# Forms of the hidden DFT matrices stored unsplit and split where the column transforms load them

## The chip, the cores and the metric

One core of one Trainium2 chip runs the kernel. The metric is device time of one execution in microseconds. The core has five engines that each work through their own list of instructions in order and wait for each other by semaphores: TensorE (PE: matmuls, PEld: its weight loads), VectorE (DVE), ScalarE (ACT), GpSimd (POOL) and SyncE (SP), whose list is mostly DMA issues.

## What is computed

```
xn = layernorm(x)                          # x: 2048 x 640, eps 1e-5, no scale or shift
a  = xn @ wr.T ;  b = xn @ wi.T            # wr, wi: 640 x 640, DFT over the hidden axis
y  = cr @ a - ci @ b                       # cr, ci: 2048 x 2048, DFT over the sequence
out = x + y + (gelu(xn @ w1 + b1) @ w2 + b2)   # w1: 640 x 1536, w2: 1536 x 640
```

All data are fp32.

## The kernel before, in words

**Split products.** TensorE takes fp32r operands. Each fp32 operand is split in two: a high half, a copy into fp32r (`high`, L189, on ScalarE), and a low half, what is left (`low`, L192, on VectorE). `product` (L301) then makes three matmuls per pair of 128-row tiles: high by high, high by low, low by high. A matmul is 128x128 weights against 128x512 columns.

**Stages.** The program runs in this order. The MLP for the first rows, then six `pair` steps (L1121), each with two hidden units of two row blocks, then the rest of the MLP. Then the sequence transform over eight blocks. Each is a Strassen-like scheme of NW = 7 products (`w` = 0 to 6) of sums of sub-blocks of cr and ci with sums of rows of xn. After the sixth and after the eighth block follows a column stage (kind "y" in `stages`, L544), which applies the hidden DFT, wr and wi, to the sums of two blocks, again as 7 products. The last column stage also takes the last four units of the MLP along with w2.

**Column stages.** A product `w` runs over ND = 5 chunks of 128 rows of its matrix form; the chunks come in the order 0, 2, 1, 3, 4. An *entry* (`hidden_entry`, L1877) handles two chunks, or one (`u` = 2), or the two late units (`u` = 3, last stage only). The matrix form of a chunk is 3 x 128 columns wide in products 0, 1, 2 and 6 and 2 x 128 in products 3, 4 and 5 (`GWIDE`), so a chunk is nine or six matmuls. The seven forms are: the first two and the last of five blocks of 128 columns of wr, then of wi, then sums of such blocks, and for product 6 the middle two of wi with the last one negated.

**Where the forms are made.** During pairs 1 to 5 and shortly after, wr and wi are loaded in five pieces (`load_w`, L397), transposed on VectorE (`turn_w`, L406), and turned into forms (`prep_w`, L447). `put_w` (L414) splits each form, ScalarE for the high half and VectorE for the low half, into a staging tile (`wst` and free tiles of other pools), and a DMA from GpSimd's queue writes both halves to DRAM (`wits`, seven tensors).

**Where they are used.** `load_g` (L1668) brings a chunk's two halves back with one DMA on SP's queue into one of 7 places (first column stage) or 13 (last): three in the tile `ws`, two each in the two `raw` tiles, which the sequence transform has left, and in the last stage six in the tiles `xab`. `hidden_entry` issues the load for a place when the chunk in it has been used, so a load is some 7 or 13 chunks ahead. Three chunks are loaded during the sequence block before the stage. No engine but TensorE touches the chunk after that.

**What sets the order.** The order is written by hand. For each entry the loop at the end of the program (L1928 on) emits the matmuls, then work left over (`later`, `pre`), then `form` for the entry three further on (a copy on ScalarE and a subtraction on VectorE, 128x1024, into one of three slots `as`, five in the last stage), then `post`: the work of `hidden_beside` (L1686) or `beside` on VectorE and ScalarE, with output DMAs. In the last column stage the outputs of three column ranges leave from GpSimd's queue (`store` with `nc.gpsimd`), and `late_form` (L1451) splits pieces of w2 on ScalarE and VectorE.

Of the kernel before, what the change touches and what calls it, by code (L numbers as in the profile page):

```python
# [15 lines left out]
P = 128  # L16
# [11 lines left out]
def kernel(  # L28
# [74 lines left out]
    ys = [dram.tile([NT, P, NB, c1 - c0], F32, name=f"ys{k}") for k, (c0, c1) in enumerate(YCOLS)]  # L103

    GWIDE = (3, 3, 3, 2, 2, 2, 3)
    wits = [dram.tile([ND, P, 2, n * P], F32, name=f"wit{w}") for w, n in enumerate(GWIDE)]
    NK = 4
    forms_ab = dram.tile([NK, P, 2, 10 * P], F32, name="forms_ab")
    forms_c = dram.tile([NK, P, 2, 7 * P], F32, name="forms_c")
# [79 lines left out]
    def high(h, s):  # L189
        nc.scalar.activation(h, s, AF.Copy)  # L190
# [220 lines left out]
            A.pop(("wraw", m)).rearrange("p (q c) i -> p q c i", q=Q),  # L411
        )

    def put_w(w, j, main, odd=None, negative=False):  # L414

        n = GWIDE[w] * P
        st, last = A["wst"], j >= ND - 2
        if w in (0, 1, 6):
            k = w % 5 if w < 6 else 2
            t = st[:, k * 6 * P : (k + 1) * 6 * P].rearrange("p (a b) -> p a b", a=2)  # L420
            parts = [(t, 0, n)]
        else:
            name = f"wst{w}_{j}"
            if w in (2, 3):
                t = rows.tile([P, 2, 2 * P], F32R, tag="yt", bufs=2, name=name)
            elif not last:
                t = early.tile([P, 2, 2 * P], F32R, tag="w2r", bufs=3, name=name)
            elif w == 4:
                t = mr.tile([P, 2, 2 * P], F32R, tag="zt" if j < ND - 1 else "ab", bufs=2, name=name)
            else:  # L430
                lo = 12 * P if j < ND - 1 else 0
                t = st[:, lo : lo + 4 * P].rearrange("p (a b) -> p a b", a=2)
            parts = [(t, 0, 2 * P)]
            if w == 2:
                parts.append((st[:, 18 * P : 20 * P].rearrange("p (a b) -> p a b", a=2), 2 * P, n))
        to = parts[-1][0][:, :, -P:]
        split(t[:, 0, : 2 * P], t[:, 1, : 2 * P], main)
        if odd is not None and not negative:
            split(to[:, 0], to[:, 1], odd)
        elif odd is not None:  # L440
            h, l = to[:, 0], to[:, 1]
            nc.scalar.activation(h, odd, AF.Copy, scale=-1.0)
            nc.vector.scalar_tensor_tensor(l, odd, -1.0, h.bitcast(F32), op0=ALU.mult, op1=ALU.subtract)
        for t, c0, c1 in parts:
            nc.gpsimd.dma_start(wits[w][j][:, :, c0:c1], t.bitcast(F32))

    def prep_w(j, k):  # L447

        (r1, r2, r4), (i1, i2, i4) = (
            (A["wt", m][:, : 2 * P], A["wt", m][:, 2 * P : 4 * P], A["wt", m][:, 4 * P :]) for m in range(2)  # L450
        )

        if k == 0:
            put_w(0, j, r1, r4)
            put_w(1, j, i1, i4)
            add(r4, r4, i4)
        if k == 1:
            put_w(6, j, i2, i4, True)
            add(i2, i2, r2)
            put_w(2, j, i2, r4)  # L460
            add(r2, r1, r2, ALU.subtract)
            add(r1, i2, r1, ALU.subtract)
            add(i1, i1, r1, ALU.subtract)
        if k == 2:
            put_w(3, j, r1)
            put_w(4, j, i1)
            put_w(5, j, r2)

    def add(dst, a, b, op=ALU.add):
        nc.vector.tensor_tensor(dst, a, b, op=op)  # L470
# [559 lines left out]
    def beside_pair(k, at):  # L1030

        if k == 0:

            if at == 5:
                bias_sum(0, 0)
                turn_x("t30", "a")
                turn_x("t31", "a")
                A["ot0"] = turn_sum(0, 0, rows, "yt", True)
                split_x("t30")
                split_x("t31")  # L1040
            if at == 6:
                turn_x("t40", "a")
                turn_x("t41", "a")
                split_x("t40")
                split_x("t41")
                bias_sum(0, 1)
                load_w(0, 0)
                load_w(1, 0)
            if at == 8:
                A["ot1"] = turn_sum(0, 1, rows, "yt", True)  # L1050
            if at == 4:
                add_sum(0, 0, A["ot0"])
                add_sum(0, 1, A["ot1"])
                store_sums(0, 0)
                bias_sum(0, 2)
            return
        j = k - 1
        if k == 1:
            if at == 2:
                add_sum(0, 2, turn_sum(0, 2, rows, "yt", True))  # L1060
            if at == 5:
                finish(0, 3, 4)
                store_sums(0, 1, 2)
            if at == 3:
                A["wst"] = zo_tile("wst", (P, NB * DQ), F32R)
        if k == LASTK and at == 4:
            split_unit(2 * NF + 1, units[1])
        if at == {1: 7, LASTK: 4}.get(k, 6):
            turn_w(0, j)
            turn_w(1, j)  # L1070
        if k == 1:
            steps = {7: (0,), 4: (1,)}
        elif k == 2:
            steps = {5: (-1,), 7: (0,), 4: (1,)}
        elif k == LASTK - 1:
            steps = {5: (-1,), 8: (0,)}
        elif k == LASTK:
            steps = {5: (-2,), 8: (-1,)}
        else:
            steps = {5: (-1,), 8: (0,), 4: (1,)}  # L1080
        if at == (7 if k == 1 else 3) and j + 1 < ND:
            load_w(0, j + 1)
            load_w(1, j + 1)
        if k == 2 and at == 2:
            home = rows_in("rt2")
            A["rows_3"] = home
            for c in range(3 * NC, 4 * NC):
                load_x(c, home=home)
        if k == LASTK - 1 and at in (7, 4):
            for c in (12, 13) if at == 7 else (14, 15):  # L1090
                ln_stats(c)
                scale_by_power(c)
        if k == LASTK and at == 8:
            split_unit(2 * NF, units[0])
        for n in steps.get(at, ()):
            prep_w(*((j - 1, 3 + n) if n < 0 else (j, n)))
        if k == LASTK and at == 2:
            for i in range(3):
                load_unit(i)
        if k == LASTK and at == 8:  # L1100
            A["gs"] = place("xab1", (P, 5, TB), F32)
            for i in range(3, 8):
                load_unit(i)
            for c in range(3 * NC, 4 * NC):
                ln_apply(c)
        if k == LASTK and at == 7:
            A["s1"] = place("xab2", (P, ND, TB), F32)
        if k == LASTK and at == 4:
            Z["z"] = place("xab3", (P, NB, DQ), F32)
            put_z(Z["z"], A["rows_3"], nc.gpsimd, nc.sync)  # L1110
            split_unit(2 * NF + 2, units[2])
# [374 lines left out]
    def beside(h, t, n):  # L1486
# [108 lines left out]
        else:  # L1595
# [12 lines left out]
                A["g", b] = [A["ws"][:, k] for k in range(3)]  # L1608
            if second and 3 <= n < 6:
                post.append(lambda: load_g(b, n - 3))  # L1610
            if n == 6 and p == 2:

                def load_yo():
                    yo[t] = out_pool.tile([P, NB, DQ], F32, tag="zo", bufs=1, name=f"yo{t}")
                    for q in range(Q):
                        nc.sync.dma_start(yo[t][q * B : (q + 1) * B], rows_of(x, t)[:, :, q * DQ : (q + 1) * DQ])

                post.append(load_yo)
# [49 lines left out]
    def load_g(b, i):  # L1668
        if i >= NW * ND:
            return  # L1670
        w, c = G[i]
        n = GWIDE[w] * P
        places = A["g", b]
        k = i % len(places)
        if b < len(blocks) - 1 and w == NW - 1:


            k = (i - 2 if c == CHUNKS[1][0] else i) % len(places)
            if c in CHUNKS[0]:
                k = CHUNKS[0].index(c)  # L1680
                places = {k: fr_tile((P, 6 * P), f"u{2 - k}_{sets[blocks[b]]}", f"gr{k}_{b}", F32R)}
        g = places[k][:, : 2 * n].rearrange("p (a b) -> p a b", a=2)
        GT[b, i] = g
        nc.sync.dma_start(g.bitcast(F32), wits[w][c])

    def hidden_beside(b, n):  # L1686

# [241 lines left out]
    for kind, what in stages:  # L1929
        b = blocks.index(what) if kind == "s" else b  # L1930
        count = NW * steps_in((kind, what)) if (kind, what) != stages[-1] else NW * NLATE
        for n in range(first, first + count):
            w, u = entries[n][2:]
            if kind == "s":
                sequence_entry(n, what, w, u)
                pre, post = beside(*what, n - first)
            else:
                hidden_entry(n, b, w, u)
                pre, post = hidden_beside(b, n - first)
            for f in later:  # L1940
                f()
            later.clear()
            for f in pre:
                f()
            while made <= n + 3 + min(max(n - LASTY + 2, 0), 2):
                form(made)
                made += 1
            for f in post:
                f()
        first += count  # L1950
        if n + 1 < len(entries):
            X, Y, Z = Y, Z, X
# [47 lines left out]
```

## Time and profile before

| | |
|---|---|
| time, median of 3 runs | 847.53 us (846.95 to 848.32) |
| the profiled execution | 847.4 us, its span 845.6 us |
| first column stage, by the timeline | 596.0 to 657.2 us |
| last column stage, by the timeline | 755.1 to 841.1 us |
| pairs and the making of the forms | about 100 to 210 us |

A row of a group names the line, the engine, the operation, the tiles (out<-in), the shapes and the count; after the bar come busy time in us, the mean of one in ns, and the idle time of that engine just before, with what ended it. A row of the timeline begins with start and duration in us. A row of the windows names the stretch, its length, and the busy time of PE, PEld, DVE, ACT and POOL with the number of instructions in brackets, the granted clock, the share of DMA and GB/s. A row of one line or tile has the shortest, median and longest duration in ns. In the waits, "A <- B: us, times, longest" says that A stood idle until B.

### The profile page before, as it was taken

The page shows a single profiled execution, that of the slowest core. Times are in us where ns is not written, and L with a number is a line of the kernel's source. Part 1 is how long each engine was busy: PE and PEld are TensorE (multiplying, and loading weights), DVE is VectorE, ACT ScalarE, POOL GpSimd, SP SyncE. Part 2 cuts the span into 40 slices and gives each one's busy share as a digit, 9 for nine tenths or more (in the row PEclk, how much of TensorE's full clock was granted, in tenths as well). Part 3 has the DMA queues.
Part 4 walks back from the last instruction along what each step waited for, and adds up shares of the span by engine and source line. Part 5 has one row for each costly group of instructions (what it writes and reads, how often), then busy time and mean ns, then how long its engine had stood idle before and what let it go on. Part 6 is the DMA issues. An engine that isn't in the chain of part 4 may idle for free.

```text
span 845.6 us, 10713 instructions
## 1 busy us (share of the span) xinstructions
PE 839.2 (99%) x3719; PEld 695.5 (82%) x3719; DVE 694.3 (82%) x920; ACT 374.6 (44%) x546; POOL 90.5 (11%) x166
## 2 busy tenths in 40 slices
PE   9999999999999999999999999999999999999997
PEld 7888888888888888888888888888888888888886
DVE  6969888778668789798988888899588998867995
ACT  7555666645547554344343432323233232344450
POOL 3340023346200000000000000000000000010102
PEclk9999999999999999999999999999999999999999
DMA  7995759889879897786534994836557997274453
GB/s 228 286 247 160 154 165 299 240 254 349 282 212 395 280 195 154 178 196 141 144 90 138 288 261 123 189 100 191 163 159 224 256 263 254 66 276 168 123 145 88
DMA packets 194454, 171.72 MB, mean 203 GB/s; under 512 B 57920, under 2 KB 164928, under 8 KB 193888
## 3 DMA queue, kind: packets, MB, share of 16 engines
q1 hardware_dynamic: 181664, 134.53, 59.4%
q0 software_dynamic: 10560, 35.99, 12.4%
q10 hardware_dynamic: 2176, 0.52, 0.3%
q8 instruction: 29, 0.48, 0.2%
q14 instruction: 25, 0.20, 0.1%
HBM read 119.87 MB, written 47.19 MB: 198 GB/s over the span
## 4 chain that ended last, share of the span: by engine, by line
PE 99%; POOL 0%; DVE 0%; issue 0%; POOLq 0%
PE banks L304 30%; PE banks L306 29%; PE banks L305 29%; PE banks L326 10%; PE banks L697 1%; PE banks L713 0%; POOL warm L685 0%; POOL zeros L683 0%; DVE yo L1961 0%; PE banks L767 0%; POOLq masks.py:199 0%; POOLq L1986 0%
## 5 line engine op out<-in xcount | busy, mean ns | idle before, releaser
L190 ACT ACTIVATE as<-r 128x1024 fp32r<-128x1024 f32 x80 | 85.0, 1062 | 170.2 <-PE banks L306 152.5
L304 PE MATMUL banks<-as,xab 128*128 128x512 f32 (+1 forms) x375 | 145.5, 388 | 0.0
L305 PE MATMUL banks<-as,xab 128*128 128x512 f32 (+1 forms) x375 | 145.5, 388 | 0.0
L306 PE MATMUL banks<-as,xab 128*128 128x512 f32 (+1 forms) x375 | 145.4, 388 | 0.0
L193 DVE TENSOR_TENSOR as<-r,as 128x1024 fp32r<-128x1024 f32 x80 | 97.1, 1215 | 38.0 <-ACT as L190 37.9
L304 PE MATMUL banks<-as,xc 128*128 128x512 f32 x244 | 94.9, 389 | 0.0
L305 PE MATMUL banks<-as,xc 128*128 128x512 f32 x244 | 94.9, 389 | 0.0
L306 PE MATMUL banks<-as,xc 128*128 128x512 f32 x244 | 94.9, 389 | 0.0
L304 PEld LDWEIGHTS banks<-as,xab 128*128 128x128 f32 x375 | 70.4, 188 | 14.6
L305 PEld LDWEIGHTS banks<-as,xab 128*128 128x128 f32 x375 | 70.4, 188 | 14.5
L306 PEld LDWEIGHTS banks<-as,xab 128*128 128x128 f32 x375 | 70.4, 188 | 14.4
L190 ACT ACTIVATE as<-rt 128x1024 fp32r<-128x1024 f32 x37 | 39.3, 1063 | 82.2 <-PE banks L306 62.7
L326 PE MATMUL banks<-xt,xab 128*128 128x512 f32 x240 | 56.6, 389 | 0.0
L193 DVE TENSOR_TENSOR as<-rt,as 128x1024 fp32r<-128x1024 f32 x37 | 44.9, 1212 | 11.7 <-ACT as L190 11.7
L304 PEld LDWEIGHTS banks<-as,xc 128*128 128x128 f32 x244 | 45.8, 188 | 9.5
L305 PEld LDWEIGHTS banks<-as,xc 128*128 128x128 f32 x244 | 45.8, 188 | 9.5
L306 PEld LDWEIGHTS banks<-as,xc 128*128 128x128 f32 x244 | 45.8, 188 | 9.5
L326 PEld LDWEIGHTS banks<-xt,xab 128*128 128x128 f32 x240 | 45.0, 188 | 9.3
L304 PE MATMUL banks<-hs,xc 128*128 128x512 f32 x120 | 46.7, 389 | 0.0
L305 PE MATMUL banks<-hs,xc 128*128 128x512 f32 x120 | 46.7, 389 | 0.0
L306 PE MATMUL banks<-hs,xc 128*128 128x512 f32 x120 | 46.7, 389 | 0.0
L1433 POOL DMA_DIRECT2D seed_x<-seeds x1 | 0.5, 543 | 382.2 <-DVE y L470 382.2
(307 smaller groups left out, 1719.3 us busy)
## 6 DMA issues: line engine op xcount, KB each, us to landing
raw<-in_A_dft_seq_re_dram SPq DMA_DIRECT2D x64, 256.0 KB, 5.2
raw<-in_A_dft_seq_im_dram SPq DMA_DIRECT2D x64, 256.0 KB, 4.9
w1r<-in_B_w_dram SPq DMA_DIRECT2D x144, 80.0 KB, 3.3
wit<-wst POOLq DMA_DIRECT2D x15, 384.0 KB, 4.4
wit<-wst POOLq DMA_DIRECT2D x20, 256.0 KB, 3.9
forms_ab<-xab SPq DMA_DIRECT2D x4, 1280.0 KB, 9.9
ws<-wit SPq DMA_DIRECT2D x13, 384.0 KB, 5.3
row<-xn SPq DMA_DIRECT2D x14, 320.0 KB, 6.0
```

The source lines that it names most:

```text
L190: nc.scalar.activation(h, s, AF.Copy)
L193: nc.vector.tensor_tensor(l, s, h.bitcast(F32), op=ALU.subtract)
L304: nc.tensor.matmul(acc, wh, mh, start=first, stop=False, skip_group_check=goes_on)
L305: nc.tensor.matmul(acc, wh, ml, start=False, stop=False, skip_group_check=goes_on)
L306: nc.tensor.matmul(acc, wl, mh, start=False, stop=last, skip_group_check=goes_on)
L326: nc.tensor.matmul(acc, W1[i][:, a, j * P : (j + 1) * P], XT[j][:, b], start=n == 0, stop=n == len(steps) - 1)
L697: nc.tensor.matmul(wacc, warm[:, :P], warm, start=True, stop=True)
L1433: nc.gpsimd.dma_start(A["seed"], seeds[:, c0:c1])
```

## The change

The forms are written to DRAM unsplit. `put_w` and the seven tensors `wits` are gone. `prep_w` writes the transposed pieces of wr and wi as they are (`wturn`) and, in one tensor `wsum`, the sums that the forms need, made by the same five additions on VectorE, and the negated block, made on ScalarE. `load_g` loads a chunk's form, in one or two DMAs (`form_of_w`), into the low half of its place. The new `split_g` makes the high half from it with ScalarE, and then subtracts the high half from the low half in place on GpSimd. It is called for the first three chunks in the block before the stage, and then at the end of each entry for chunks up to four ahead of those that the entry used (five, behind the last entry of a product).

```diff
     GWIDE = (3, 3, 3, 2, 2, 2, 3)
-    wits = [dram.tile([ND, P, 2, n * P], F32, name=f"wit{w}") for w, n in enumerate(GWIDE)]
+    wturn = dram.tile([ND, P, 2, D], F32, name="wturn")
+    wsum = dram.tile([ND, P, 10 * P], F32, name="wsum")
...
-    def put_w(w, j, main, odd=None, negative=False):
...
-        split(t[:, 0, : 2 * P], t[:, 1, : 2 * P], main)
-        if odd is not None and not negative:
-            split(to[:, 0], to[:, 1], odd)
-        elif odd is not None:
-            h, l = to[:, 0], to[:, 1]
-            nc.scalar.activation(h, odd, AF.Copy, scale=-1.0)
-            nc.vector.scalar_tensor_tensor(l, odd, -1.0, h.bitcast(F32), op0=ALU.mult, op1=ALU.subtract)
-        for t, c0, c1 in parts:
-            nc.gpsimd.dma_start(wits[w][j][:, :, c0:c1], t.bitcast(F32))
...
+        st = A["wst"][:, j % 2 * 10 * P :][:, : 10 * P]
+        n4, s2, s4, d1, t1, e1 = (
+            st[:, lo * P : (lo + w) * P] for lo, w in ((0, 1), (1, 2), (3, 1), (4, 2), (6, 2), (8, 2))
+        )
 
         if k == 0:
-            put_w(0, j, r1, r4)
-            put_w(1, j, i1, i4)
-            add(r4, r4, i4)
+            for m in range(2):
+                nc.gpsimd.dma_start(wturn[j][:, m], A["wt", m])
+            nc.scalar.activation(n4, i4, AF.Copy, scale=-1.0)
         if k == 1:
-            put_w(6, j, i2, i4, True)
-            add(i2, i2, r2)
-            put_w(2, j, i2, r4)
-            add(r2, r1, r2, ALU.subtract)
-            add(r1, i2, r1, ALU.subtract)
-            add(i1, i1, r1, ALU.subtract)
+            add(s2, i2, r2)
+            add(s4, r4, i4)
+            add(d1, r1, r2, ALU.subtract)
         if k == 2:
-            put_w(3, j, r1)
-            put_w(4, j, i1)
-            put_w(5, j, r2)
+            add(t1, s2, r1, ALU.subtract)
+            add(e1, i1, t1, ALU.subtract)
+            nc.gpsimd.dma_start(wsum[j], st)
+
+    def form_of_w(w, c):
+
+        r, i, st = wturn[c][:, 0], wturn[c][:, 1], wsum[c]
+        two, odd = slice(0, 2 * P), slice(4 * P, D)
+        return (
+            (r[:, two], r[:, odd]),
+            (i[:, two], i[:, odd]),
+            (st[:, P : 4 * P],),
+            (st[:, 6 * P : 8 * P],),
+            (st[:, 8 * P :],),
+            (st[:, 4 * P : 6 * P],),
+            (i[:, 2 * P : 4 * P], st[:, :P]),
+        )[w]
...
+            if second and 8 <= n < 11:
+                post.append(lambda: split_g(b, n - 7))
...
-        nc.sync.dma_start(g.bitcast(F32), wits[w][c])
+        lo = 0
+        for src in form_of_w(w, c):
+            cols = slice(lo, lo + src.shape[-1])
+            nc.sync.dma_start(g[:, 1, cols].bitcast(F32), src)
+            lo = cols.stop
+
+    split_to = {}
+
+    def split_g(b, stop):
+
+        for i in range(split_to.get(b, 0), min(stop, NW * ND)):
+            h, l = (GT[b, i][:, k] for k in range(2))
+            high(h, l.bitcast(F32))
+            nc.gpsimd.tensor_tensor(l, l.bitcast(F32), h.bitcast(F32), op=ALU.subtract)
+        split_to[b] = max(stop, split_to.get(b, 0))
...
             for f in post:
                 f()
+            if kind == "y":
+                done = w * ND + (min(2 * u + 2, ND) if u < 3 else ND)
+                split_g(b, done + (4 if u < 3 else ND))
```

The lines of the changed program are counted anew: L190, L470 and L1684 of before are L191, L453 and L1672 there.

**ScalarE at the start of the first column stage**, before (`as` are the slots of forms, `u` and `v` the sums that the forms are made from):

```order
L190 ACTIVATE as<-u_0_3_4057 128x1024
L190 ACTIVATE as<-u_3_3964 128x512
L190 ACTIVATE as<-v_0_3_4185 128x1024
L190 ACTIVATE as<-v_0_3_4012 128x1024
L190 ACTIVATE as<-v_3_4183 128x512
L190 ACTIVATE as<-u_1_0_4406 128x1024
```

And now (`ws`, `gr_a` and `gr_b` are places of chunks):

```order
L191 ACTIVATE as<-u_0_3_3904 128x1024
L191 ACTIVATE as<-u_3_3811 128x512
L191 ACTIVATE as<-v_0_3_4032 128x1024
L191 ACTIVATE gr_a_4638<-gr_a_4638 128x384 x2
L191 ACTIVATE gr_b_4639<-gr_b_4639 128x384
L191 ACTIVATE as<-v_0_3_3859 128x1024
L191 ACTIVATE gr_b_4639<-gr_b_4639 128x384
L191 ACTIVATE ws<-ws 128x384
L191 ACTIVATE as<-v_3_4030 128x512
L191 ACTIVATE ws<-ws 128x384
```

The form copies stand in the same order; the copies of chunks have come between them, those of the fourth, fifth and sixth chunk behind the first form copy of the stage.

**GpSimd from the MLP's end through the first column stage**, before:

```order
L1017 DMA seeds<-s_2229 128x1024 x2
L1017 DMA seeds<-s_2229 128x512
L616 DMA xc_2623<-xn 128x640 x2
L1433 DMA seed_x<-seeds 128x1024
L1433 DMA seed_y<-seeds 128x1024
```

And now, its first rows:

```order
L599 DMA xc_2470<-xn 128x640 x2
L1682 TENSOR_TENSOR ws<-ws 128x384 x3
L1682 TENSOR_TENSOR gr_a_4638<-gr_a_4638 128x384 x2
L1682 TENSOR_TENSOR gr_b_4639<-gr_b_4639 128x384 x2
L1682 TENSOR_TENSOR ws<-ws 128x384 x3
L1682 TENSOR_TENSOR gr_a_4638<-gr_a_4638 128x384 x2
L1682 TENSOR_TENSOR gr_b_4639<-gr_b_4639 128x384 x2
L1682 TENSOR_TENSOR ws<-ws 128x384
L1682 TENSOR_TENSOR ws<-ws 128x256 x2
L1682 TENSOR_TENSOR gr_a_4638<-gr_a_4638 128x256 x2
```

GpSimd had no instruction in that stage; it now has 35 subtractions.

**GpSimd in the last column stage**, before (`out_dram` are output DMAs, `late_units` and `seeds` loads):

```order
L1446 DMA rt_5753<-late_units 128x1024 x3
L1638 DMA xc_5805<-seeds 128x1024
L1433 DMA seed_z<-seeds 128x1024
L1375 DMA out_dram<-yo_5357 32x16x32 x4
L1375 DMA out_dram<-u_1_2_5417 32x16x64 x4
L1375 DMA out_dram<-y_2_5655 32x16x32 x4
```

And now, from the middle of the stage to the end:

```order
L1682 TENSOR_TENSOR ws<-ws 128x256
L1358 DMA out_dram<-yo_5289 32x16x32 x4
L1682 TENSOR_TENSOR gr_b_5679<-gr_b_5679 128x256 x2
L1682 TENSOR_TENSOR gr_a_5680<-gr_a_5680 128x256 x2
L1682 TENSOR_TENSOR xab_2298<-xab_2298 128x256 x3
L1682 TENSOR_TENSOR xab_2355<-xab_2355 128x256 x3
L1682 TENSOR_TENSOR ws<-ws 128x256 x3
L1682 TENSOR_TENSOR gr_b_5679<-gr_b_5679 128x256
L1358 DMA out_dram<-u_1_2_5349 32x16x64 x4
L1682 TENSOR_TENSOR gr_b_5679<-gr_b_5679 128x384
L1682 TENSOR_TENSOR gr_a_5680<-gr_a_5680 128x384 x2
L1682 TENSOR_TENSOR xab_2298<-xab_2298 128x384 x2
```

The output DMAs, which wait for VectorE, now stand between the subtractions of chunks that are still to be used.

More of the change, by code (lines that the diff above doesn't have):

```diff
@@ L412, in turn_w @@
         )
-    def put_w(w, j, main, odd=None, negative=False):
[L416 to L436, printed above, removed]
-        split(t[:, 0, : 2 * P], t[:, 1, : 2 * P], main)
-        if odd is not None and not negative:
-            split(to[:, 0], to[:, 1], odd)
-        elif odd is not None:
-            h, l = to[:, 0], to[:, 1]
-            nc.scalar.activation(h, odd, AF.Copy, scale=-1.0)
-            nc.vector.scalar_tensor_tensor(l, odd, -1.0, h.bitcast(F32), op0=ALU.mult, op1=ALU.subtract)
-        for t, c0, c1 in parts:
-            nc.gpsimd.dma_start(wits[w][j][:, :, c0:c1], t.bitcast(F32))
     def prep_w(j, k):
@@ L1064, in beside_pair @@
             if at == 3:
-                A["wst"] = zo_tile("wst", (P, NB * DQ), F32R)
+                A["wst"] = zo_tile("wst", (P, NB * DQ))
         if k == LASTK and at == 4:
```

## The prediction

> **What bounds the kernel now.** I read the page first, then the waits of the tensor engine alone, then the chain in order of time.
>
> ```profile
> span 845.6 us, 10713 instructions
> PE 839.2 (99%) x3719; PEld 695.5 (82%) x3719; DVE 694.3 (82%) x920; ACT 374.6 (44%) x546; POOL 90.5 (11%) x166
> PE 99%; POOL 0%; DVE 0%; issue 0%; POOLq 0%
> PE banks L697 <- POOL warm L685: 2.0, 1, 2.0
> 24.90 3.40 PE banks L326 x15
> 841.22 0.45 DVE yo L1961
> ```
>
> The chain that ended last is 99% TensorE, and the only wait that TensorE has in the whole program is 2.0 us for its first warm-up operand. Fifteen matmuls take 3.40 us, 0.227 us each, and that spacing holds to the end. The last transposition and its store follow at 841.22 us. So nothing that is taken off another engine can be won: the change keeps every matmul, and the front and the tail, as they are. What it can do is make TensorE wait where it never did. I work against the profiled execution, 847.4 us, of which the span is 845.6; the median of the three runs is 847.53, the same within 0.02%.
>
> **The change part by part.** In the preparation the split copies go.
>
> ```profile
> L190 ACT ACTIVATE wst<-row 128x256 fp32r<-128x256 f32 x35 | 13.5, 408 | 10.6 <-DVE row L470 5.0 <-DMA ys<-xo 2.8 <-DMA wit<-wst 2.6
> L193 DVE TENSOR_TENSOR wst<-row,wst 128x256 fp32r<-128x256 f32 x35 | 14.0, 420 | 10.3 <-ACT wst L190 10.3
> L193 DVE TENSOR_TENSOR wst<-row,wst 128x128 fp32r<-128x128 f32 x15 | 4.3, 284 | 0.0
> L443 DVE SCALAR_TENSOR_TENSOR wst<-row,wst 128x128 fp32r<-128x128 f32 x5 | 1.4, 285 | 0.0
> wit<-wst POOLq DMA_DIRECT2D x15, 384.0 KB, 4.4
> wit<-wst POOLq DMA_DIRECT2D x20, 256.0 KB, 3.9
> ```
>
> VectorE loses 14.0 + 4.3 + 1.4 = 19.7 us, ScalarE a similar amount, and the writes shrink from 15 x 384 + 20 x 256 KB = 10.9 MB to ten of 320 KB and five of 640 KB, 6.4 MB. All of it stood beside a TensorE that did not wait: worth 0. The loads in the column stages halve in bytes, and 15 of 35 become two issues each; their queue waits on buffers now, and I cost the extra issues at 0 because a load is issued seven chunks or more ahead of its use. If that cover were gone, each would delay its chunk by the issue alone.
>
> What is added is 35 copies on ScalarE and 35 in-place subtractions on GpSimd in each of the two column stages, and these stand on the path: a chunk's matmuls can't start without them. In a stage 20 chunks are 384 wide and 15 are 256 wide.
>
> ```profile
> L780 POOL TENSOR_TENSOR xab<-w1r,xab x1: 1003/1003/1003, 10.4 to 10.4; 128x384 fp32r<-128x384 f32 x1
> L641 ACT ACTIVATE xab<-row 128x384 fp32r<-128x384 f32 x14 | 6.6, 511 | 1.7 <-DMA row<-xn 1.7
> L641 ACT ACTIVATE xab<-row 128x256 fp32r<-128x256 f32 x7 | 2.8, 401 | 0.0
> 595.96:657.16 61.20, 61.20 (x272) 50.68 (x271) 48.87 (x49) 20.38 (x22) 0.00 (x0) 1.00 0.62 197
> 755.08:841.13 86.05, 86.05 (x400) 71.99 (x398) 70.06 (x94) 32.16 (x49) 8.30 (x13) 1.00 0.50 154
> ```
>
> The last two rows are the two column stages (us, then busy PE, PEld, DVE, ACT, POOL). ScalarE gets 20 x 0.51 + 15 x 0.40 = 16.2 us in each, on 20.4 of 61.2 and 32.2 of 86.05: room enough. GpSimd has one row like its new work, 1.003 us at 384 wide. The 256-wide one is not in the trace; it lies between 0.67 (in proportion) and 1.00, and I take 0.70, near the proportional end since the 384 row is the same operation. So GpSimd gets 20 x 1.003 + 15 x 0.70 = 30.6 us in each stage. By its own total it would fit as well. Two things can still stop TensorE.
>
> **First, the order.** Splits are emitted after an entry's other work and only four chunks ahead.
>
> ```profile
> 600.23 1.06 ACT L190 ACTIVATE as<-v 128x1024 fp32r<-128x1024 f32 x1 [4.81 <-PE banks L306]
> L190 ACT ACTIVATE xc<-xab 128x256 fp32r<-128x256 f32 x8 | 3.0, 403 | 0.0
> L190 ACT ACTIVATE xc<-xab 128x128 fp32r<-128x128 f32 x4 | 1.2, 294 | 0.0
> L1721 ACT ACTIVATE v<-banks 128x1024 f32<-128x1024 f32 x2 | 2.0, 1018 | 1.4 <-DVE as L193 1.4
> L1375 POOL DMA_DIRECT2D out_dram<-yo x4 | 2.6, 662 | 33.2 <-DVE yo L470 33.2
> L1375 POOL DMA_DIRECT2D out_dram<-u x4 | 2.6, 649 | 23.8 <-DVE u L470 23.8
> ```
>
> Only three chunks are split before a stage begins. The fourth, needed in the middle of the second entry, stands on ScalarE behind the form copy that waits for the end of the first entry (600.23 to 601.29). Its own copy ends at 601.8 and GpSimd at 602.8. The second entry starts at 595.96 + 18 x 0.227 = 600.04; it wants this chunk after six matmuls, 601.4, and its low half two later, 601.85. So TensorE waits some 1.0 us. In the last stage four copies for the late units stand ahead (2 x 0.40 + 2 x 0.29 = 1.4): 2.4 us. At the end of each stage the seventh product first spends only three matmuls, 0.68 us, on a chunk, where GpSimd needs 1.0: four times 0.32 is 1.3 us, in each stage. ScalarE's copy at L1721 waits 1.4 us for VectorE and takes 1.0, and now has two chunks behind it: between 0 and 2.4, I take 2.0. Two groups of four output DMAs, 2.6 us each, stand in front of splits on GpSimd in the last stage: between 0 and 5.2, I take 3.4, since both are at points with little lead. Sum: 1.0 + 2.4 + 2.6 + 2.0 + 3.4 = 11.4 us, bounds 5 to 17.
>
> **Second, whether GpSimd and VectorE can work at once.** The trace has no two-operand GpSimd operation beside a two-operand VectorE operation in SBUF. It has these:
>
> ```profile
> L727 POOL TENSOR_TENSOR mv<-mv,eps x4: 570/617/810, 5.3 to 8.1; 128x1 f32<-128x1 f32 x4
> L1026 POOL TENSOR_TENSOR mv<-mv,eps x4: 567/568/572, 180.4 to 183.8; 128x1 f32<-128x1 f32 x4
> 7.05 1.35 POOL L727 TENSOR_TENSOR mv<-mv,eps 128x1 f32<-128x1 f32 x2
> 7.76 0.60 DVE L240 TENSOR_SCALAR xp<-row,mv 128x640 f32<-128x640 f32 x1
> 10.52 1.45 DVE L193 TENSOR_TENSOR xt<-banks,xt 128x384 fp32r<-128x384 f32 x3 [0.22 <-ACT xt L190]
> ```
>
> One power on GpSimd took 810 ns where the others take 570: it ended at 7.05 + 1.35 = 8.40, just behind the VectorE operation from SBUF to SBUF that ended at 7.76 + 0.60 = 8.36. It looks held until that was over. Beside L780 (10.38 to 11.38) VectorE read one operand from PSUM, and its three operations took their usual 1.45 us. So exclusion, for operations that read SBUF on both engines, has one row for it and none against it. The Trainium skill, in "SBUF — State Buffer", section "SBUF: two separate sides", states it as a rule: the two engines share one port pair, taken as an exclusive lock for a whole instruction, by a VectorE operation with two SBUF inputs against a GpSimd operation that reads SBUF. By that rule the form subtractions of VectorE and the new subtractions of GpSimd take turns; the 810 ns row agrees, and no run here shows the pair itself.
>
> If they take turns throughout, the two engines' work adds up. First stage: 48.9 + 30.6 = 79.5 us against 61.2 of matmuls, 18.2 over. Last stage: 70.1 + 30.6 = 100.7 against 86.05, 14.6 over. Together 32.8 us. From below: what reads PSUM or a single operand can go on beside GpSimd.
>
> ```profile
> L470 DVE TENSOR_TENSOR v<-v,banks 128x1024 f32<-128x1024 f32 x3 | 3.6, 1214 | 0.0
> L1397 DVE STREAM_TRANSPOSE yb<-v 128x1024 f32<-128x1024 f32 x2 | 2.5, 1246 | 0.1
> L1397 DVE STREAM_TRANSPOSE ya<-banks 128x1024 f32<-128x1024 f32 x2 | 2.5, 1242 | 0.0
> L531 DVE STREAM_TRANSPOSE rt<-raw 128x1024 f32<-128x1024 f32 x1 | 1.2, 1235 | 0.0
> L1394 DVE STREAM_TRANSPOSE yo<-banks 128x512 f32<-128x512 f32 x1 | 0.7, 707 | 0.0
> L470 DVE TENSOR_TENSOR v<-v,banks 128x512 f32<-128x512 f32 x1 | 0.7, 681 | 0.0
> ```
>
> That is 11.2 us in the first stage, which leaves 7.0 over; I estimate as much or a little more for the last, which leaves nothing over there. With the 11.4 us of order this is 18.4, so 866. From above, all turns and all of the order: 32.8 + 11.4 = 44.2, so 892. The middle is 31; I take the plain sum of turns, 32.8, because VectorE works in order and rarely has a free operation at hand when it is held, while part of the 11.4 us falls into the same waits. 847.4 + 32.8 = 880.2 us.
>
> **The rivals.** *The engines work side by side and only the order costs*: 847.4 + 11.4 = 858.8 us, 853 to 864 by the bounds. For it: no pair of this kind is in the trace, and one stretched power is thin. Against: VectorE is at 80% of both stages, so even a partial hold would show. *Everything is hidden, not slower*: a split costs 0.5 + 1.0 us, and four chunks of lead are 4 x 9 x 0.227 = 8.2 us in a wide product and 5.4 in a narrow one. If ScalarE and GpSimd kept that lead from the first chunk on, the time would stay at 847.4. This decides at the fourth chunk: it holds if its copy is done before 601.4, and the row at 600.23 speaks against it. *The loads land too late* would come on top, 880 and more, but halved bytes and seven chunks of lead speak against it; it has no chance of its own. Faster would need a wait to go, and TensorE has none but the first.
>
> **How the numbers follow.** Turns between GpSimd and VectorE 0.61 (880, 866 to 892), order alone 0.30 (859), hidden 0.07 (847), faster by something unseen 0.02. The likeliest gives 880. The range takes both of the first two with their bounds, 854 to 892, and leaves out about 0.17. About 0.2%, 1.7 us, is what a measurement of this kernel can tell from no change; slower by more than that 0.91, within it 0.07, faster 0.02.
>
> **What would show it.** TensorE waits that name GpSimd's subtraction, in the two column stages and nowhere else, 15 to 25 us in the first and 10 to 20 in the last. With turns, the GpSimd subtractions beside VectorE are longer than 1.0 us, or form subtractions of 128x1024 are longer than 1.22 us, or their starts alternate; without turns both keep these durations and the waits sum to about 11. The preparation, 120 to 210 us, shows less VectorE and ScalarE work and the same number of matmuls. I am wrong if TensorE waits outside the column stages, or for a load.

## The result, and the profile after

| | before | after |
|---|---|---|
| time, median | 847.5 us (846.92 to 848.32, 6 runs) | 876.29 us (871.97 to 877.84, 6 runs) |
| the profiled execution | 847.4 us, span 845.6 | 871.97 us, span 870.2 |
| first column stage, first matmul to first matmul behind it | 61.2 us | 72.3 us |
| last column stage, first to last matmul | 85.8 us | 99.9 us |

The ratio is 1.0329, with a 95% interval of 1.0301 to 1.0357: the change makes the kernel 29 us slower. The profiled execution is the fastest of the six, 4 us below their median. Its granted clock was 0.996, and the three longest executions, 877.11 to 877.84 us, had 0.992. So some 4 us of the median are not in the trace that I read here.

The page of the kernel after comes first: span, busy time of each engine, and the chain that ended last by engine.

```profile
span 870.2 us, 10835 instructions
PE 848.1 (97%) x3719; PEld 695.6 (80%) x3719; DVE 703.8 (81%) x865; ACT 387.6 (45%) x566; POOL 162.8 (19%) x211
PE 83%; issue 6%; POOL 5%; DVE 3%; DMA 2%; SPq 1%; ACT 0%; POOLq 0%; DVEq 0%; ACTq 0%
```

The matmuls are the same 3719. VectorE has 55 instructions fewer and is nevertheless 9.5 us busier. The chain, 99% TensorE before, now passes through GpSimd and VectorE. Which instructions TensorE waited for is in its waits:

```profile
PE banks L307 <- POOL gr_b L1682: 4.5, 4, 3.5
PE banks L305 <- ACT gr_b L191: 4.0, 2, 2.8
PE banks L305 <- DVE v L453: 3.3, 1, 3.3
PE banks L680 <- POOL warm L668: 2.0, 1, 2.0
PE banks L307 <- POOL gr_a L1682: 1.9, 2, 1.0
PE banks L307 <- POOL xab L1682: 0.8, 2, 0.5
PE banks L307 <- POOL gr L1682: 0.6, 1, 0.6
```

Apart from the old wait for `warm`, all of them lie in the two column stages. Most name a chunk's copy (L191) or its subtraction (L1682); one, of 3.3 us, names a VectorE sum. These waits come to some 15.5 of the 25 us that the two stages lost in this execution. The rest lies in gaps of 0.1 to 0.3 us behind them and in matmuls at half rate (last section). The windows show where time was lost and where it wasn't (us, length, then busy PE, PEld, DVE, ACT, POOL, the granted clock, the share of DMA, GB/s): the preparation, the stretch behind it, and the two column stages with a few tenths of a us around them.

```profile
100.00:210.00 110.00, 110.00 (x487) 91.07 (x486) 74.44 (x144) 51.91 (x86) 31.91 (x57) 1.00 0.76 220
210.00:590.00 380.00, 380.00 (x1678) 314.67 (x1677) 318.70 (x354) 162.65 (x210) 8.61 (x14) 1.00 0.73 193
595.74:668.06 72.32, 66.08 (x272) 50.98 (x270) 60.00 (x49) 31.97 (x54) 43.31 (x32) 0.98 0.35 102
765.98:866.10 100.12, 90.55 (x400) 72.45 (x398) 83.08 (x94) 43.50 (x80) 44.36 (x45) 0.98 0.34 99
```

From 100 to 590 us TensorE has no gap, 487 and 1678 matmuls. In the column stages VectorE has the same 49 and 94 instructions as before, but takes 60.00 us for them instead of 48.87, and 83.08 instead of 70.06. GpSimd's 30 us of new work read 43 and 36 us (44.36 less the 8.3 that it had). Both engines are longer over the same work, as if each waited inside its instructions for the other; e2 and e4 below show that this is so. A stretch of the timeline of the last column stage shows how (start, duration):

```profile
830.39 4.53 POOL L1682 TENSOR_TENSOR ws<-ws 128x256 fp32r<-128x256 f32 x3
830.90 1.75 DVE L194 TENSOR_TENSOR r<-u,r 128x1024 fp32r<-128x1024 f32 x1
...
832.58 1.75 DVE L453 TENSOR_TENSOR rt<-rt 128x1024 f32<-128x1024 f32 x1
...
834.26 1.74 DVE L194 TENSOR_TENSOR r<-u,r 128x1024 fp32r<-128x1024 f32 x1
...
835.92 1.21 DVE L453 TENSOR_TENSOR v<-banks,xc 128x1024 f32<-128x1024 f32 x1
```

Three VectorE operations of 1.22 us take 1.75, 1.75 and 1.74, and three subtractions, 0.73 us each where nothing is beside them, take 4.53: they alternate, one subtraction in each VectorE operation. The last row reads PSUM and has its usual 1.21. TensorE's wait of 3.3 us for `v` ends just behind it, at 837.28.

It isn't always one for one. When GpSimd comes back from its four output DMAs in that stage, four subtractions are due:

```profile
815.51 3.51 DVE L453 TENSOR_TENSOR u<-u,u 128x512 f32<-128x512 f32 x1
815.65 1.42 POOL L1682 TENSOR_TENSOR gr_b<-gr_b 128x256 fp32r<-128x256 f32 x2
...
817.02 1.44 POOL L1682 TENSOR_TENSOR gr_a<-gr_a 128x256 fp32r<-128x256 f32 x2
```

They run through at their usual 0.74 us each, and a VectorE sum that takes 0.68 us alone takes 3.51: one operation lost 2.83 us to four. At the same place in e3, below, three in a row make it 2.82 us. So subtractions that fall due together hold VectorE longer.

### The profile page after: what moved, and what is told of

It reads as the page before. It is cut to its first block, busy times and chain, and to the rows that moved or that the text cites. A ratio compares the mean times of both kernels' runs of the same rounds, so it can differ in the third digit from the quotient of the medians.

```text
span 870.2 us, 10835 instructions
## 1 busy us (share of the span) xinstructions
PE 848.1 (97%) x3719; PEld 695.6 (80%) x3719; DVE 703.8 (81%) x865; ACT 387.6 (45%) x566; POOL 162.8 (19%) x211
## 3 DMA queue, kind: packets, MB, share of 16 engines
HBM read 108.08 MB, written 41.94 MB: 172 GB/s over the span
## 4 chain that ended last, share of the span: by engine, by line
PE 83%; issue 6%; POOL 5%; DVE 3%; DMA 2%; SPq 1%; ACT 0%; POOLq 0%; DVEq 0%; ACTq 0%
PE banks L307 25%; PE banks L305 24%; PE banks L306 24%; PE banks L327 9%; POOL gr_b L1682 1%; POOL xab L1682 1%; POOL gr_a L1682 1%; POOL ws L1682 1%; DVE as L194 1%; SPq L1672 0%; DMA row<-in_A_x_dram 0%; DMA u<-ys 0%; DMA xab<-wsum 0%; DVE xab L453 0%; DMA ws<-wsum 0%
## 5 line engine op out<-in xcount | busy, mean ns | idle before, releaser
L191 ACT ACTIVATE as<-r 128x1024 fp32r<-128x1024 f32 x80 | 85.0, 1062 | 172.0 <-PE banks L307 148.0
L1682 POOL TENSOR_TENSOR ws<-ws 128x384 fp32r<-128x384 f32 (+1 forms) x24 | 31.6, 1328 | 321.4 <-DVE u L453 297.3
L191 ACT ACTIVATE as<-rt 128x1024 fp32r<-128x1024 f32 x37 | 39.3, 1062 | 76.9 <-PE banks L307 61.2
```

Source lines behind the costliest of these rows:

```text
L1682: nc.gpsimd.tensor_tensor(l, l.bitcast(F32), h.bitcast(F32), op=ALU.subtract)
```

## The experiments

Two mechanisms stood in the prediction: the *order* (a split is emitted so late that its chunk isn't ready, however long the operations take) and the *turns* (GpSimd's and VectorE's operations hold each other). The first four runs below take them apart. The ratios are to the kernel before in the same series, 847.71 us beside e1 to e4, 848.47 beside e5 and e6, 848.2 beside e7.

| run | time, us | ratio [95%] | first stage | last stage |
|---|---|---|---|---|
| before | 847.5 | | 61.2 | 85.8 |
| after | 876.29 | 1.0329 [1.0301, 1.0357] | 72.3 | 99.9 |
| e2, nothing read, order kept | 858.30 | 1.0123 [1.0108, 1.0139] | 64.9 | 92.4 |
| e3, larger lead, reading kept | 870.11 | 1.0263 [1.0247, 1.0279] | 69.4 | 99.1 |
| e5, nothing read, larger lead | 851.85 | 1.0037 [1.0015, 1.0058] | 62.7 | 87.8 |
| e4, turns in the kernel before | 858.43 | 1.0128 [1.0111, 1.0145] | 66.5 | 89.4 |
| e1, subtraction on VectorE | 885.72 | 1.0442 [1.0417, 1.0467] | 80.0 | 102.1 |
| e6, two multiplications by 0 | 912.59 | 1.0759 [1.0736, 1.0781] | 98.0 | 115.0 |
| e7, one multiplication by 0 | 866.52 | 1.0208 [1.0191, 1.0225] | 72.4 | 94.0 |

### e2: the order alone

```diff
-            nc.gpsimd.tensor_tensor(l, l.bitcast(F32), h.bitcast(F32), op=ALU.subtract)
+            for _ in range(2):
+                nc.gpsimd.memset(l.bitcast(F32), 0.0)
```

> The changed kernel, with each GpSimd subtraction replaced by two GpSimd fills of the low half with zeros: the same waits, the same place in GpSimd's list and about the same length (2 x 0.45 us at 384 wide), but nothing is read from SBUF; the low halves of the matrix forms are left out of the result. Turns, if it is the reading that excludes: VectorE's durations go back to 1.22 us, what is left is the order, 11 us by the prediction's sum, so 856 to 862. Order alone: about the changed kernel's 872 to 878.

Measured: 858.30 us (857.42 to 859.04). The windows of its two column stages:

```profile
596.05:660.99 64.94, 63.24 (x272) 50.06 (x271) 48.97 (x49) 31.89 (x54) 22.62 (x64) 1.00 0.40 113
758.90:851.48 92.58, 88.27 (x400) 71.39 (x398) 70.25 (x94) 43.52 (x80) 31.16 (x77) 1.00 0.37 106
```

VectorE is back at 48.97 and 70.25 us with the same instructions, so nothing holds it beside an operation that only writes. The order is untouched, and costs 858.30 - 847.5 = 10.8 us. What is left of the 28.8, 18.0 us, came with the subtraction in place of the fills. Not all of it need be its reading: two fills take 0.84 us at 384 wide and 0.62 at 256, the subtraction alone 1.01 and 0.73. My estimate for this is 0.17 us at each of the nine waits that name a subtraction in the kernel after, some 1.5 us.

### e3: the splits emitted earlier

```diff
-                split_g(b, done + (4 if u < 3 else ND))
+                ahead = 9 if b == len(blocks) - 1 else 5
+                split_g(b, min(done + ahead, len([1 for bb, i in GT if bb == b])))
```

> The changed kernel with the splits emitted further ahead: five chunks in the first column stage instead of four, nine in the last, as far as the chunks have been loaded. Turns: VectorE and GpSimd have as much work as before, so most of the loss stays, 868 to 876, though waits at single chunks shrink. Order alone: with the lead doubled in the last stage most of its waits go, and the time falls to 850 to 860.

Measured: 870.11 us (868.39 to 871.63). In the first stage the kernel after leads by four chunks behind every entry; its five behind the last entry of a product come in the last stage alone, where `u` reaches 3. TensorE's waits in it:

```profile
PE banks L306 <- DVE as L194: 5.0, 5, 2.1
PE banks L305 <- DVE v L453: 4.8, 1, 4.8
PE banks L305 <- ACT gr_b L191: 2.5, 2, 1.2
...
PE banks L307 <- POOL gr_a L1682: 1.0, 1, 1.0
PE banks L307 <- POOL gr_b L1682: 0.4, 1, 0.4
```

With more lead the waits for GpSimd fall from 7.8 us to 1.4, but TensorE now waits 9.8 us for VectorE: for its forms and its sum `v`. A longer lead hides GpSimd's slowness and not VectorE's, whose busy time in the last stage is 89.09 us here against 83.08 in the kernel after. The lead wins 6.2 us; with the fills it wins 858.30 - 851.85 = 6.5 (e5). It takes away only a part of the order's 10.8 us in either case.

### e5: both taken away

e2's and e3's edits together.

> Both terms taken away at once: the fills of e2_memset, which read nothing from SBUF (the low halves are left out of the result), with the lead of e3_ahead (five and nine chunks). If turns and order are the whole loss, little is left: the chunk behind the first form copy in each stage can't be had earlier, 1 us and 2 us, and some at single copies, so 849 to 854. If a third thing costs time (more issues for the loads, the extra copies on ScalarE), the time stays near e2_memset's 858.

Measured: 851.85 us (850.89 to 852.82) beside 848.47 for the kernel before in the same series. Above 0.3 us only four waits are left, at the fourth chunk of each stage: 0.36 and 0.39 us, 1.38 and 0.39 us. Order and turns together are the whole loss, but for 3.4 us, of which 3.0 are these stage starts with the small gaps behind them, which the larger lead doesn't reach.

### e4: turns without the change

The kernel before, with reads of chunks by GpSimd into a tile that nobody uses, called where the change calls its splits.

```diff
+            for c0 in range(0, h.shape[-1], P):
+                nc.gpsimd.tensor_tensor(idle, l[:, c0 : c0 + 120], h[:, c0 : c0 + 120], op=ALU.subtract)
```

> The kernel before, unchanged in everything that TensorE uses, with 90 extra GpSimd subtractions of 128x120 in each column stage (three for each wide chunk, two for each narrow one), which read the two halves of a chunk and write a tile that nobody reads. Turns between GpSimd and VectorE: the extra work, some 0.4 us each and 36 us a stage, delays VectorE's form subtractions although nothing waits for GpSimd's result; single VectorE subtractions of 128x1024 grow from 1.22 to 1.6 us or more, TensorE waits for them, and the time rises by 5 to 20 us, 853 to 868. Order alone: nothing that TensorE needs stands behind the extra work, so the time stays within 1 us of 847.5 and VectorE's durations stay at 1.22 us.

Measured: 858.43 us (857.74 to 859.32). A piece of the timeline in the first column stage (L193 and L470 are the form's subtraction and the sums in this program):

```profile
631.29 4.92 POOL L1695 TENSOR_TENSOR padr<-gr_a 128x120 f32<-128x120 f32 x4
631.69 1.46 DVE L470 TENSOR_TENSOR u<-u,u 128x1024 f32<-128x1024 f32 x1
633.07 1.46 DVE L193 TENSOR_TENSOR as<-v,as 128x1024 fp32r<-128x1024 f32 x1
634.45 1.45 DVE L470 TENSOR_TENSOR u<-u,u 128x1024 f32<-128x1024 f32 x1
```

No matmul waits for the result of these 128x120 subtractions, which take 0.44 us alone. They lengthen each VectorE operation from 1.22 to 1.46 us, less than the 1.6 that I expected, and are themselves stretched to 1.23. VectorE's busy time in the stages rises from 48.87 to 55.13 and from 70.06 to 79.74 us. Turns therefore cost time without any of the change's order. The longest wait of TensorE, 3.3 us in the last stage, shows the way it goes:

```profile
825.32 1.21 DVE L470 TENSOR_TENSOR v<-banks,xc 128x1024 f32<-128x1024 f32 x1
826.63 0.47 PE L304 MATMUL banks<-r,xab 128*128 128x512 f32 x1 [3.29 <-issue]
```

The profile names no releaser ("issue"), but the matmul starts 0.1 us behind the end of VectorE's sum `v`, at the place where TensorE waits for `v` in the kernel after too. How much of the 10.7 us is turns is less clean: a place's next load now waits until GpSimd has read it, and 2.9 us of TensorE's waits name such loads.

### e1: the subtraction on VectorE

```diff
-            nc.gpsimd.tensor_tensor(l, l.bitcast(F32), h.bitcast(F32), op=ALU.subtract)
+            nc.vector.tensor_tensor(l, l.bitcast(F32), h.bitcast(F32), op=ALU.subtract)
```

> The changed kernel with the subtraction of split_g on VectorE instead of GpSimd: no two engines compete, but VectorE gets 20 x 0.55 + 15 x 0.42 = 17 us more in each column stage, 66 of 61.2 us in the first and 87 of 86 in the last. Turns: about as slow as the changed kernel, 862 to 878, since there VectorE was held for much the same time. Order alone, with GpSimd's longer instruction as its main term: faster than the changed kernel by at least 5 us, except that VectorE's list then is the limit.

Measured: 885.72 us (882.51 to 887.15), above what I expected. The window of the first stage, and two groups in it (line, engine, operation, shapes, count, then busy us, mean ns, idle before):

```profile
596.36:676.35 79.99, 67.43 (x271) 51.16 (x270) 62.92 (x82) 31.86 (x54) 0.00 (x0) 0.96 0.32 95
...
L194 DVE TENSOR_TENSOR as<-v,as 128x1024 fp32r<-128x1024 f32 x6 | 7.3, 1224 | 8.6 <-ACT as L191 8.6
...
L1682 DVE TENSOR_TENSOR gr_b<-gr_b 128x384 fp32r<-128x384 f32 x6 | 3.3, 544 | 0.0
```

A subtraction is faster here (0.54 us at 384 wide), nothing is held, and VectorE is busy for only 62.9 of 80 us. I had counted busy time. What costs is the list: VectorE works in order, and now stands behind ScalarE's copies of chunks and of forms (8.6 us before one group alone), so an operation that could run waits behind one that can't. Beside that, 27 matmuls ran at half rate (below). That GpSimd's turns cost less than this, 876 against 886, says that the remedy "give it to VectorE" is none.

### e6 and e7: an operation with one operand

```diff
-            nc.gpsimd.tensor_tensor(l, l.bitcast(F32), h.bitcast(F32), op=ALU.subtract)
+            for _ in range(2):
+                nc.gpsimd.tensor_scalar(l, l.bitcast(F32), 0.0, None, op0=ALU.mult)
```

> The changed kernel, with each GpSimd subtraction replaced by two GpSimd multiplications of the low half by zero in place: one operand is read from SBUF instead of two (the low halves are left out of the result). If a single read on GpSimd is enough to exclude VectorE's two-operand work, VectorE's busy time in the first column stage lies well above 49 us, and the time between e2_memset's 858 and the changed kernel's 876 or above. If it takes two operands on both sides, as in e2_memset: VectorE at 49 us and 856 to 861.

Measured: 912.59 us (910.77 to 915.28), far from both. The size of the operation was wrong: alone it takes 1.17 us at 384 wide and 0.845 at 256, so two per chunk are 20 x 2 x 1.17 + 15 x 2 x 0.845 = 72 us in a stage of 61.2 us of matmuls. GpSimd alone now had more work than the stage has matmuls, so the run's time tells nothing on operands. Its VectorE rows do: the longest of 128x1024 take 1.53 us, as in e7. e7 takes the operation once.

> The subtraction of a chunk's low half is replaced by one GpSimd in-place multiplication by 0 (one operand read, one written); low halves are left out. One such operation took 1.17 us at 384 wide and 0.845 us at 256 in the run with two of them, so GpSimd gets 20 x 1.17 + 15 x 0.845 = 36 us in each column stage, which fits into 61.2 and 86.05 us; this time GpSimd is not the bound by itself. If any GpSimd operation that reads SBUF takes turns with VectorE's two-operand operations: as with the subtraction or a little more, 868 to 882 us, 128x1024 subtractions of VectorE up to 2 us, GpSimd operations up to 2 us. If only a GpSimd operation with two operands does: VectorE's rows keep 1.22 us, its busy time in the stages 48.9 and 70.1 us, and the time is that of the order alone with a slightly longer operation, 858 to 863 us.

Measured: 866.52 us (864.89 to 867.92), between the two expectations: neither holds as I put it. Its groups of VectorE's and GpSimd's operations (shortest, median, longest in ns, first and last start):

```profile
L453 DVE TENSOR_TENSOR rt<-rt x20: 1180/1218/1526, 314.6 to 828.5; 128x1024 f32<-128x1024 f32 x20
...
L1683 POOL TENSOR_SCALAR ws<-ws x24: 846/1292/1929, 582.9 to 833.3; 128x384 fp32r<-128x384 f32 x13, 128x256 fp32r<-128x256 f32 x11
```

and the same two in the kernel after:

```profile
L453 DVE TENSOR_TENSOR rt<-rt x20: 1182/1218/2042, 312.7 to 832.6; 128x1024 f32<-128x1024 f32 x20
...
L1682 POOL TENSOR_TENSOR ws<-ws x24: 731/1184/1992, 581.2 to 833.2; 128x384 fp32r<-128x384 f32 x13, 128x256 fp32r<-128x256 f32 x11
```

GpSimd is held as before, up to 1.93 us. VectorE is held too, but shorter: at most 1.53 - 1.22 = 0.31 us for an operation of 1.17 us, where the subtraction of 1.01 us took 2.04 - 1.22 = 0.82 us from it. So a one-operand operation of GpSimd does take turns, at a smaller price for VectorE, though it is the longer of the two. By stage the run has two faces: the first stage is 72.4 us long, as with the subtraction (72.3), the last 94.0, near e2's 92.4. How much of this is GpSimd's longer operation (36 us in each stage against 30.6) and how much the turns is not settled. It does show that a stage's length doesn't follow VectorE's busy time: VectorE is busy for 53.03 us in the first stage here and for 60.00 in the kernel after, and the stage is equally long.

No version that was tried with the forms stored unsplit beats the kernel before. e3's order is the better one for this change, 6 us below it.

## Why the prediction was right, and which sizes were off

**The bound and the terms at nothing.** That TensorE had no wait to lose, and that the preparation is worth 0, held: VectorE is 14.1 us less busy between 100 and 210 us (88.53 to 74.44), ScalarE 12.4, and TensorE is at 110.00 of 110.00 with 487 matmuls in both. The loads' extra issues cost nothing: no wait of TensorE names a load, while the bytes read fell from 119.87 to 108.08 MB.

**The order, 11.4 us forecast, 10.8 measured** (e2 against before). Its parts, by e2's waits above 0.3 us: the first stage's start 0.36 + 0.39 = 0.75 (1.0 forecast), the copy behind VectorE 1.40 (2.0), the last stage's start 1.38 + 0.39 = 1.77 (2.4), the splits behind the output DMAs 1.73 + 1.02 = 2.75 (3.4). The seventh products came to 0.9 in the last stage and nothing in the first (2.6 for both), but a memset pair there is shorter than a subtraction. Each part was a little high: together they are 7.6 us. What made up the sum were small gaps behind the waits, of 0.1 to 0.2 us, which I hadn't counted, so that the two sums agree is partly luck. In the kernel after, where an order's wait meets a held VectorE, the same places are longer: 2.97 us at the copy at L1720, 3.66 at the first output DMAs.

**The turns.** The mechanism was right. The rival "order alone" is refused by e2, which keeps the order and changes what GpSimd reads (and, by 0.1 to 0.2 us a chunk, how long it takes), and by e4, where nothing waits for GpSimd's results; "hidden" is refused by all. My one row for exclusion was thinner than I read it: of the four powers, two were longer, 810 and 661 ns, and the VectorE operation beside both has one tensor operand, so it said nothing on the pair that mattered. The size was off, in one step: the plain addition 48.9 + 30.6 = 79.5 us for the first stage, 18.2 over its matmuls. That stage took 72.3, 11.1 more than before. The step erred in two ways that the profile shows:

- It let every subtraction stand in VectorE's way. VectorE lost 60.00 - 48.87 = 11.1 us in all, against 30.6. Operations that read PSUM, a transposition in SBUF (0.71 us at 849.97, as without GpSimd), and the gaps in which VectorE waits for ScalarE let GpSimd pass. I had this as the bound from below, 7.0 us over, and argued it away with "rarely has a free operation at hand".
- It took the whole subtraction as held time. A held VectorE operation mostly loses 0.53 us to one that lasts 0.73, and 0.82 to one of 1.01; the exception is the sum that lost 2.83 us to four.

The lower bound is no better a rule. For the first stage it gives 7.0, and 7.0 with an order of 1.0 + 1.3 + 2.0 = 4.3 is 11.3, what was measured; but for the last it leaves nothing, and the turns cost as much there. The last stage was 14.05 us longer in the profile, near the 14.6 of the plain addition, but not by its mechanism: 6.5 of them are order (92.4 in e2 against 85.8). After less e2, the turns are 7.4 us in the first stage and 7.5 in the last, 2.8 of them matmuls at half rate, which no term of mine had. By the medians they are 18.0 in all; the 3 us between lie in executions that have no trace. VectorE was busy for 60.00 of 72.3 us and 83.08 of 99.9, so it never ran out of time as a whole. What cost was single results that came late.

So 876.29 stands for 847.5 + 10.8 + 18.0, where I had 847.4 + 32.8 with the order taken as inside the turns. That 880 lies within 4 us of it is partly luck: the addition was 7 us too high in the first stage, and in the last the order, which I had left out of the sum, made up for turns half as large. The two do not share waits to a degree that shows. Each beside the kernel before in its own series, turns cost 28.8 - 10.6 = 18.2 us with the order (after less e2), and 22.4 - 3.4 = 19.0 with the larger lead (e3 less e5); the single runs of the kernel after spread by 6 us. Waits that name GpSimd's subtraction, where I forecast "15 to 25 us in the first and 10 to 20 in the last", came to 3.0 and 4.8; only with all that TensorE lost, 11.1 and 14.05, does the last stage fall into its range, and the first doesn't. And some of the waits named VectorE's sum `v`, not GpSimd: a held VectorE is late for TensorE as well, which I hadn't listed.

## What to carry to other kernels

Moving an elementwise operation to an idle engine is free only if the two engines can work at the same time: count which operations of the busy engine read two operands from SBUF, since here only those were seen held. Adding up busy times doesn't size the loss: it gave 18 us for the first stage with all operations and 7 with the held ones alone, and 15 and nothing for the last; the turns cost 7.4 and 7.5. Look instead for the results that TensorE needs soonest, and for places where several of the new operations fall due at once. Work put into the path of an engine without a single wait needs a lead at every point, and the places to look are stage starts, instructions that wait for a third engine, and DMA issues that wait in the same list. Taking reading away (a memset) and taking lateness away (a larger lead), alone and together, separates the two causes with three runs, and whether the effects add up can be read from all four corners.

## What the runs showed of the hardware that was not expected

**Half-rate matmuls behind some waits.** The timeline of TensorE behind its wait in the first column stage of the kernel after:

```profile
636.49 0.50 PE L305 MATMUL banks<-as,gr_b 128*128 128x512 f32 x1 [2.81 <-ACT gr_b L191]
...
639.13 0.63 PE L305 MATMUL banks<-as,gr_b 128*128 128x512 f32 x1
639.56 0.63 PE L306 MATMUL banks<-as,gr_b 128*128 128x512 f32 x1
639.99 0.63 PE L307 MATMUL banks<-as,gr_b 128*128 128x512 f32 x1
```

Matmuls start 0.43 us apart instead of 0.227. There are 14 such in this execution, 7 each behind gaps of 2.97 and 3.46 us (beyond the usual spacing) and none behind the longest, 3.66 us: at 0.2 us each 2.8 us of the loss. The granted clock is 0.50 there, both times for 3.41 us; the first:

```profile
637.39:640.80 3.41, 3.41 (x8) 2.68 (x9) 3.08 (x3) 1.84 (x5) 3.28 (x4) 0.50 0.10 29
```

e1 had 27 of them in three groups, e3 8 behind a gap of 5.01 us, e7 one group of 7 behind gaps of 1.87 and 0.37 us, and e6 several groups. e2, e5 and e4 had none, e4 in spite of a gap of 3.46 us. The executions with a lower granted clock were also the longer ones, which is why I put the spread of the kernel after down to this; only the profiled execution shows the matmuls themselves. The Trainium skill, in "TensorE: Matmul & The Clock Gate", section "What's actually happening", has the clock halve after an idle window of about 3.4 us that runs freely, regardless of when work starts. The rows agree in the halving and in that the length of a gap alone doesn't decide. But the gaps of 2.97 us here and of 1.87 and 0.37 us in e7 are shorter than that window, so what sets the clock back stays open.

**A hold is shorter than the instruction.** VectorE lost 0.24 us to a GpSimd subtraction 120 wide (0.44 us alone), 0.53 at 256 (0.73), 0.82 at 384 (1.01): some 0.2 us of each subtraction ran beside it. Four at 256 in a row cost it 2.83 (4 x 0.74). For the multiplication at 384 wide it lost 0.31 of 1.17. The Trainium skill, in "SBUF — State Buffer", section "SBUF: two separate sides", has the lock held for the whole instruction; the turns agree with it, these differences don't.

**A one-operand operation that is slower than one with two.** GpSimd's multiplication by a constant, in place, takes 1.17 us at 128x384 and 0.845 at 128x256, its subtraction of two tiles 1.01 and 0.73.
